# A recurrent attention block and a maxout layer on one core: all engine and load orders laid anew

## The chip, the core and the metric

The kernel runs on one core of a Trainium2 chip. A core has TensorE (PE, matrix products, with its weight loads shown apart as PEld), VectorE (DVE), ScalarE (ACT), GpSimd (POOL) and SyncE (SP, which only issues transfers here). The metric is the device time of one execution in microseconds; the median of three runs of the kernel before is 131.71 us (131.47 to 132.38).

## The reference

Two stages. The first is a gated linear recurrence for 4 batches of 8 heads, 768 steps, head size 48:

```
for t in range(768):
    state = alpha[:, :, t, :, None] * state + einsum('bhd,bhe->bhde', k[:, :, t], v[:, :, t])
    y[:, :, t] = einsum('bhd,bhde->bhe', q[:, :, t], state)
```

Its output, laid out as x with 3072 rows of 384, goes through a layer with 1024 hidden columns:

```
g = maximum(x @ w1, x @ w2)
out = g @ w_out
```

## The kernel before

The 768 steps are cut into chunks of 128, and two chunks of one batch (256 steps) are a *unit*; there are 12 units. The recurrence becomes matrix products: cumulated logarithms of alpha turn q and k into scaled forms, the scores inside a chunk are one masked product, and what older chunks give comes through a running state. The maximum is computed as x @ w2 + relu(x @ (w1 - w2)), so that the second product needs two parts: relu(...) @ w_out and x @ (w2 @ w_out), where w2 @ w_out is computed once at the start.

Names of the steps, with u the unit (units 0 and 1 are cut into two halves of four heads, .0 and .1) and their lines:

- `ld.*` (L346, L368, transposes L515): loads that SP issues; af, qf, kf, vf are alpha, q, k, v of a unit, w2, wo, w1 pieces of the weights. Units 4 to 6 and 11 use the weights' staging space.
- `lg`, `sg`, `ra` (L457 to L465): logarithm of alpha, sum of a step pair, exponential. `cs` (PE, L480, L482): cumulated sums. `em`, `ep`, `de` (ACT, L485 to L489): their exponentials.
- `k0`, `q0`, `kn`, `qn` (L415, L497, L502): scaled k and q. `tp` (PE, L527): their transposes, `qk` (L418): the copy out of PSUM. For units 10 and 11 transposing transfers on SP take the place of both.
- `pp` (PE, L553): scores; `pt` (DVE, L565, L570): scores times the mask.
- `kv` (PE, L602), `tm` (DVE, L635, L637), `dd`, `sb` (L621, L415): update of the running state. `vc`, `w` (L418): copies of v; `dm` (L588): decay factors.
- `y` (PE, L663): output of the recurrence; `xt` (L418): its copy out of PSUM.
- `wt` (PE, L383), `wtc`, `woc` (L418), `wq` (PE, L405), `wqc` (L409): w2 transposed, w_out cast, and the 24 products of w2 @ w_out. `w12` (L399): w1 - w2, in four column groups.
- `h` (PE, L693), `g` (L698 on DVE, L699 on ACT): the hidden product, four column groups per unit, and its relu. `o` (PE, L720), `oc` (L418), `st` (L730, L735): the output product, copy and store (ACT issues it).

Many steps can run on more than one of ACT, DVE and POOL; many helpers share one line (copies L418, products L415).

The order of the work is written out by hand: `ORDERS` holds for each of PE, ACT, DVE, POOL and SP the list of step names in the sequence in which that engine runs them, and with it on which engine a step runs. `Plan.follow` steps through these lists with a duration for every step and constants for latencies, tile-shape switches and instruction fetches. It doesn't reorder anything; from its reckoned times come the PSUM bank that each result takes (`where`), the sequence in which instructions are emitted, and the gaps of PE in its first 45 us, into which `fill` (L840) emits products of a zero tile:

```
while left > 0.06:
    cols = min(512, int(600 * left / slow) - 3)
    nc.tensor.matmul(env["PB"][b][:, 0:cols], lhsT=w[:, 0:128], rhs=w[:, 0:cols], start=True, stop=True)
```

Waits between engines follow from the data. The tile shapes of PE products are three: whole array, A (64 rows: tp, pp, kv) and C (32 columns: y).

Of the kernel before, what the change touches and what calls it, by code (L numbers as in the profile page):

```python
# [201 lines left out]
o1.0.x0 cs4 h2.3 h2.0 h2.2 pp3 cs5 o2.1.x0 o2.0.x0 o2.0.f0 h2.1 o2.1.f0 y3 tpk4 tpq4 o2.1.f1 o2.0.f1 o2.0.f2
o2.1.f2 h3.3 pp4 o2.1.f3 h3.0 h3.2 o2.0.f3 h3.1 tpq5 kv5 tpk5 kv4 o3.0.x0 cs6 o3.0.f0 o3.1.x0 o3.1.f0 o3.0.f1
o3.1.f1 o3.1.f2 o3.1.f3 o3.0.f2 y4 pp5 o3.0.f3 h4.0 h4.3 h4.2 h4.1 y5 tpk6 tpq6 kv6 cs8 cs7 h5.0 o4.0.x0 o4.0.f0
h5.1 o4.0.f1 o4.0.f2 o4.1.x0 o4.0.f3 o4.1.f0 o4.1.f1 tpq7 pp6 tpk7 o4.1.f2 o4.1.f3 h5.3 o5.0.x0 h5.2 o5.0.f0
o5.0.f1 y6 tpk8 tpq8 kv7 o5.0.f2 o5.0.f3 o5.1.x0 o5.1.f0 pp7 o5.1.f1 cs9 h6.0 o5.1.f2 o5.1.f3 h6.2 h6.3 y7 tpq9
tpk9 pp8 o6.1.x0 h6.1 o6.1.f0 h7.3 h7.1 o6.1.f1 kv8 kv9 pp9 o6.1.f2 h7.0 h7.2 o7.0.x0 o7.1.x0 y8 y9 cs10 o7.0.f0
o6.0.x0 o6.0.f0 cs11 o7.1.f0 o7.1.f1 o6.0.f1 h8.2 o7.0.f1 o8.0.x0 o7.0.f2 o6.1.f3 h8.0 o7.0.f3 o7.1.f2 o6.0.f2
h8.1 o6.0.f3 h9.0 h8.3 o8.0.f0 o8.1.x0 h9.3 o7.1.f3 o8.1.f0 h9.1 o8.0.f1 o8.0.f2 kv10 pp10 o8.1.f1 o9.1.x0
o8.1.f2 o8.1.f3 o9.1.f0 o8.0.f3 h9.2 y10 kv11 pp11 o9.1.f1 o9.0.x0 o9.0.f0 o9.1.f2 h10.0 o9.0.f1 o9.0.f2  # L210
o10.0.x0 o10.1.x0 o9.1.f3 o10.0.f0 y11 o10.1.f0 o9.0.f3 h10.2 h10.1 h10.3 h11.0 o10.0.f1 h11.3 h11.1 o10.1.f1
# [11 lines left out]
qk8.1 oc5.0 lg10 vc8 w7.01 em9 ep9 de9 g6.0 g6.2 g6.3 xt7.0 xt7.1 w9.00 qk9.1 w10.11 g6.1 g7.3 st4 g7.1 w9.01
w10.00 st5 lg11 g7.0 w9.10 ra10 ra11 g7.2 xt8.1 de10 xt8.0 em10 ep10 em11 vc11 g8.2 ep11 de11 g8.0 g9.0 w10.10
g8.3 oc6.1 g9.3 g9.1 oc8.1 w11.11 xt10.1 st6 w11.00 g10.0 xt11.0 xt11.1 oc9.1 g11.0 st7 g10.2 g10.3 st8 g11.1
g11.3 oc9.0 st9 st10 oc11.0 st11.0 oc11.1 st11.1 st11.2
# [3 lines left out]
q00.0 qn0.1 kn0.0 qn0.0 kn1.0 k01.1 q01.0 pt0.1.1 qn1.1 qn1.0 pt0.1.0 qk1.0.1 pt0.0.1 tm1.0 pt1.0.0 pt1.0.1  # L230
pt0.0.0 pt1.1.0 tm0.0 pt1.1.1 tm1.1 wtc.20 tm0.1 xt0.1 xt1.1 w12.1 wtc.01 zsb0 w12.2 sg2 w12.3 zsb2 g0.2 g0.3
kn2 g1.3 q02 qn2 dm3 q03 qn3 qk2.0 w2.01 k03 tm2.0 pt2.0 pt2.1 qk3.0 tm3.0 xt2.1 tm2.1 qk3.1 oc1.0 q04 tm3.1
pt3.0 pt3.1 qn4 xt3.0 k05 dm5 sg6 qk4.0 qn5 pt4.0 pt4.1 oc2.1 g3.2 g3.1 tm5.0 tm4.0 sb5.1 sg7 qk5.0 qk5.1 tm5.1
tm4.1 xt4.1 pt5.1 pt5.0 qn6 g4.3 oc3.0 tm6.0 g4.2 qk6.0 qn7 tm6.1 qk6.1 oc4.0 qn8 pt6.0 pt6.1 oc4.1 g5.2 g5.3
# [644 lines left out]
```

## Time and profile before

| | |
|---|---|
| median of 3 runs | 131.71 us |
| profiled execution: span | 129.8 us |
| median less that span | 1.9 us |
| PE busy | 124.4 us (96%) |
| of it fills (L840) | 10.6 us |
| DVE, ACT, POOL busy | 98.6, 96.8, 70.7 us |
| mean granted TensorE clock | 0.999 |
| read from HBM, written | 23.59 MB, 4.72 MB |

The profiled execution's own time beside its span isn't in the profile: the span runs from its first to its last instruction, and what lies around it is taken as the 1.9 us between the span and the median. Busy time of PE comes from matmuls whose ends are modelled, and fills count in it. A row of the stretches gives start and end, length, then the busy time and count of PE, PEld, DVE, ACT and POOL, the granted clock, the share of DMA time and GB/s. A row of the chain of waits gives start, length, engine, tile and line. Rows of the timeline have start, length, engine, line, operation, tiles, shapes, count, and in brackets idle time before it with what ended it.

### The profile page before, as it was taken

The page shows a single profiled execution, that of the slowest core. Times are in us where ns is not written, and L with a number is a line of the kernel's source. Part 1 is how long each engine was busy: PE and PEld are TensorE (multiplying, and loading weights), DVE is VectorE, ACT ScalarE, POOL GpSimd, SP SyncE. Part 2 cuts the span into 40 slices and gives each one's busy share as a digit, 9 for nine tenths or more (in the row PEclk, how much of TensorE's full clock was granted, in tenths as well). Part 3 has the DMA queues.
Part 4 walks back from the last instruction along what each step waited for, and adds up shares of the span by engine and source line. Part 5 has one row for each costly group of instructions (what it writes and reads, how often), then busy time and mean ns, then how long its engine had stood idle before and what let it go on. Part 6 is the DMA issues. An engine that isn't in the chain of part 4 may idle for free.

```text
span 129.8 us, 4785 instructions
## 1 busy us (share of the span) xinstructions
PE 124.4 (96%) x1987; PEld 88.5 (68%) x1987; DVE 98.6 (76%) x177; ACT 96.8 (75%) x199; POOL 70.7 (54%) x112
## 2 busy tenths in 40 slices
...
GB/s 76 325 325 357 414 371 346 344 273 294 232 314 309 262 275 250 318 272 315 301 314 337 251 287 340 202 230 135 5 13 91 105 89 39 121 5 14 258 167 167
DMA packets 60837, 29.66 MB, mean 229 GB/s; under 512 B 54672, under 2 KB 60432, under 8 KB 60816
## 3 DMA queue, kind: packets, MB, share of 16 engines
...
q10 hardware_dynamic: 3424, 4.72, 10.0%
q8 instruction: 15, 0.25, 0.7%
q14 instruction: 6, 0.05, 0.1%
HBM read 23.59 MB, written 4.72 MB: 218 GB/s over the span
## 4 chain that ended last, share of the span: by engine, by line
PE 79%; ACT 9%; DMA 5%; issue 2%; DVE 2%; SPq 0%; ACTq 0%
PE pb L720 28%; PE pb L693 20%; PE pb L840 8%; PE pb L663 6%; DMA af<-in_alpha_dram 5%; PE pb L527 4%; PE pb L553 3%; PE pb L405 3%; PE pb L602 3%; ACT w L418 2%; PE pb L480 1%; ACT ra L465 1%; PE pb L383 1%; ACT gt L699 1%; ACT lg L457 1%
## 5 line engine op out<-in xcount | busy, mean ns | idle before, releaser
L720 PE MATMUL pb<-wo,gt 128*128 128x384 f16 (+2 forms) x200 | 39.8, 320 | 0.0
L693 PE MATMUL pb<-xt,w 128*128 128x256 f16 x288 | 36.7, 272 | 0.1
L693 PEld LDWEIGHTS <-w 128*128 128x128 f16 x288 | 27.9, 98 | 6.5 <-issue 0.4
L699 ACT ACTIVATE gt<-pb 128x512 f16<-128x512 f32 x35 | 20.2, 595 | 9.7 <-PE pb L693 9.1
L565 DVE TENSOR_TENSOR pt<-pb,mask 128x1024 f16<-128x1024 f32 x20 | 23.5, 1217 | 1.9 <-PE pb L553 1.9
L720 PEld LDWEIGHTS <-gt 128*128 128x128 f16 x200 | 18.1, 98 | 9.1
L415 POOL TENSOR_TENSOR sb<-tm,dd 128x384 f16<-128x384 f32 x15 | 12.4, 830 | 9.0 <-DVE tm L635 8.7
L698 DVE TENSOR_SCALAR gt<-pb 128x512 f16<-128x512 f32 x13 | 8.7, 680 | 9.0 <-PE pb L693 9.0
L720 PE MATMUL pb<-w2o,xt 128*128 128x384 f16 (+2 forms) x75 | 15.3, 320 | 0.0
L840 PE MATMUL pb<-wsrc 128*128 128x512 f32 (+6 forms) x18 | 10.6, 709 | 1.5 <-DVE wsrc L846 1.5
L418 ACT CAST xt<-pb 128x384 f16<-128x384 f32 x15 | 8.3, 592 | 4.4 <-PE pb L663 4.3
L635 DVE TENSOR_TENSOR tm<-pb,sb 128x384 f32<-128x384 f32 x16 | 8.6, 550 | 3.6 <-PE pb L602 2.9
L418 DVE COPY os<-pb 128x384 f32<-128x384 f32 (+1 forms) x13 | 6.9, 531 | 4.7 <-PE pb L720 4.5
L418 ACT COPY os<-pb 128x384 f32<-128x384 f32 (+1 forms) x12 | 5.6, 468 | 6.4 <-PE pb L720 5.9
L418 ACT COPY qk<-pb 128x512 f16<-128x512 f16 (+1 forms) x13 | 9.9, 781 | 0.3 <-PE pb L527 0.2
L663 PE MATMUL pb<-pt,w 128*32 128x128 f16 x384 | 10.1, 220 | 0.0
L663 PEld LDWEIGHTS <-w 128*32 128x32 f16 x384 | 8.3, 96 | 2.5 <-issue 1.9
L418 ACT CAST w<-vf 64x384 f16<-64x384 f32 x19 | 9.7, 509 | 0.3
L497 POOL TENSOR_TENSOR kn<-kf,em 128x768 f16<-128x768 f32 (+1 forms) x5 | 8.3, 1650 | 2.6 <-PE pb L553 1.9
L720 PEld LDWEIGHTS <-xt 128*128 128x128 f16 x75 | 6.9, 98 | 4.0
L663 PE MATMUL pb<-qk,sb 128*32 128x128 f16 x240 | 9.5, 219 | 0.0
L457 ACT ACTIVATE lg<-af 128x768 f16<-128x768 f32 (+1 forms) x10 | 6.9, 710 | 3.3 <-DMA af<-in_alpha_dram 3.0
...
## 6 DMA issues: line engine op xcount, KB each, us to landing
out_dram<-os ACTq DMA_DIRECT2D x11, 384.0 KB, 3.0
af<-in_alpha_dram SPq DMA_DIRECT2D x8, 384.0 KB, 6.5
kf<-in_k_dram SPq DMA_DIRECT2D x8, 384.0 KB, 5.8
qf<-in_q_dram SPq DMA_DIRECT2D x8, 384.0 KB, 5.2
vf<-in_v_dram SPq DMA_DIRECT2D x8, 384.0 KB, 5.4
...
wof<-in_moe_w_out_dram SPq DMA_DIRECT2D x4, 384.0 KB, 7.5
w1f<-in_moe_w_dram SPq DMA_DIRECT2D x4, 384.0 KB, 9.2
```

Source lines behind the costliest of these rows:

```text
L415: return lambda: getattr(nc, e).tensor_mul(out=o(), in0=x(), in1=y())
L418: return lambda: nc.scalar.copy(out=o(), in_=i()) if e == "scalar" else getattr(nc, e).tensor_copy(out=o(), in_=i())
L457: add(f"lg{nq}", "ACT", lambda h_=h_: nc.scalar.activation(out=V("LG")[lg][:, :, h_].rearrange("p r h d -> p h r d"), in_=AFn()[:, h_], fu ...
L497: eng.tensor_mul(out=V(nm)[i3][:, :, h_, 0:D], in0=rhd(src())[:, :, h_], in1=bc(fac()))
L565: f = lambda e=e: nc.vector.tensor_mul(out=V("PT")[pt][:, e].rearrange("p a j x -> p (a j) x"), in0=pair(pp[e][0]).rearrange("p n (j x) -> ...
L635: nc.vector.tensor_add(out=V("TM")[new], in0=kvv, in1=V("SB")[m4])
L663: nc.tensor.matmul(o, lhsT=l, rhs=r, start=(a, qd) not in seen, stop=i == len(todo[qd]) - 1, skip_group_check=True)
L693: nc.tensor.matmul(t[:, m, :], lhsT=V("w12")[:, ds, f * 128 : f * 128 + 128], rhs=V("XT")[x3][:, ds, :], start=(ds == 0), stop=(ds == ND - 1))
L698: gd = lambda g2=g2, v2=v2: nc.vector.tensor_relu(out=g2(), in_=v2())
L699: ga = lambda g2=g2, v2=v2: nc.scalar.activation(out=g2(), in_=v2(), func=ACTF.Relu)
L720: nc.tensor.matmul(b32(x, w), lhsT=l, rhs=r, start=fst and y_ == 0, stop=lst and y_ == len(ws) - 1)
L840: nc.tensor.matmul(env["PB"][b][:, 0:cols], lhsT=w[:, 0:128], rhs=w[:, 0:cols], start=True, stop=True)
```

## The change

The five lists in `ORDERS` are replaced by others with the same steps. Every PE step and every load is in both, in another sequence; ACT has 202 entries where it had 212, DVE 176 where it had 165, POOL 100 where it had 101. The constants in `Plan` by which the lists are reckoned change as well: the switch between tile shapes depends on the pair of shapes, an instruction fetch delays the load queue by up to 0.6 us some time after it's asked for, a store's issue takes 0.42 us of ACT where it took 0.1, and some durations differ by a few hundredths. Operations, tiles and data types are as before.

At the start, PE has these steps ahead of the first h: before, nine of the 24 wq, with y1 and y0 in front of all of them; after, eighteen wq, seven of them in front of y0 and y1. The load list puts all four wo pieces ahead of w1.0. `w12.0` moves from POOL to DVE, `sb1.1` from POOL to DVE, `sg1.0` and `k01.0` too. The relu `g` goes from 35 on ACT and 13 on DVE to 27 and 21; output copies from 12 and 13 to 18 and 7; `xt` from 15 and 9 to 19 and 5; of the 48 copies `w`, ACT makes 22 and POOL 23 where they made 32 and 14.

```diff
-    SWITCH = 0.096
+    SWITCH = {"u": 0.112, "A": 0.128, "C": 0.148, "uC": 0.1}
...
-    FETCH = 0.85
+    FETCH = 0.6
+    BACKLOG = (25.0, 3.0, 1.2)
...
     "PE": """
-cs0.1 cs1.1 cs1.0 cs0.0 tpk0.1 tpq0.1 tpq0.0 tpk0.0 pp0.1 tpq1.1 tpk1.0 tpq1.0 tpk1.1 kv1 pp0.0 wt.11 pp1.0
-wt.10 wt.01 pp1.1 kv0 wt.00 wt.21 wt.20 y1.0 y1.1 y0.0 y0.1 wq.10 wq.20 wq.11 wq.21 wq.00 wq.01 wq.22 wq.12
-wq.02 h0.0 h1.0 wq.23 h0.1 h1.1 o1.1.f0 wq.13 h0.2 h1.2 cs2 o1.1.f1 o0.1.f0 wq.03 wq.24 o0.1.f1 h0.3 wq.14 wq.15
...
+cs1.1 cs0.1 cs0.0 cs1.0 tpk0.1 tpq0.1 tpq0.0 tpk0.0 pp0.1 kv0 tpq1.0 tpk1.0 pp0.0 wt.20 tpk1.1 tpq1.1 kv1 wt.21
+wq.20 wt.00 pp1.1 pp1.0 wq.21 wt.10 wt.01 wt.11 wq.00 wq.01 wq.22 wq.02 wq.23 y0.0 y0.1 y1.0 y1.1 wq.03 wq.24 wq.10
+wq.25 wq.26 wq.04 wq.11 wq.12 wq.05 wq.13 wq.06 h1.0 h0.0 wq.27 h1.1 o1.0.f0 h1.2 wq.14 h0.2 o1.1.f0 wq.07 wq.15 cs2
...
     "DVE": """
...
+q00.1 k00.0 qn0.1 qn0.0 kn0.0 qk0.1.0 k01.0 k01.1 kn1.0 pt0.1.1 tm0.0 pt0.1.0 qn1.0 qn1.1 qk1.0.0 pt0.0.0 pt0.0.1
+qk1.1.0 tm1.0 tm0.1 pt1.1.0 pt1.0.0 pt1.1.1 pt1.0.1 sb1.1 woc.5 woc.4 w12.0 zkn2 w12.1 w12.2 g1.2 sg2 tm1.1 g0.2
...
     "SP": """
-ld.af0 ld.af1 ld.kf0 ld.qf0 ld.kf1 ld.vf1 ld.qf1 ld.vf0 ld.w2.1 ld.w2.0 ld.wo.0 ld.w2.2 ld.w1.0 ld.wo.1 ld.w1.1
-ld.w1.2 ld.af2 ld.wo.2 ld.w1.3 ld.kf2 ld.af3 ld.wo.3 ld.qf2 ld.qf3 ld.vf2 ld.kf3 ld.vf3 ld.af4 ld.af5 ld.qf4
...
+ld.af1 ld.af0 ld.kf0 ld.qf0 ld.vf0 ld.kf1 ld.qf1 ld.vf1 ld.w2.2 ld.wo.0 ld.w2.0 ld.w2.1 ld.wo.1 ld.wo.2 ld.wo.3
+ld.w1.0 ld.w1.1 ld.w1.2 ld.af2 ld.af3 ld.w1.3 ld.kf2 ld.qf2 ld.qf3 ld.vf2 ld.kf3 ld.vf3 ld.af4 ld.qf4 ld.kf4 ld.af5
```

More of the change, by code (lines that the diff above doesn't have):

```diff
@@ L80, in follow @@
         count, block, pe = 0, 189, 1.2
-        nblock, avail = 0, 0.0
+        nblock, avail, due = 0, 0.0, []
+        wait = lambda at: due.append(at + self.BACKLOG[1 if at < self.BACKLOG[0] else 2])
         def ready(o):
@@ L149, in follow @@
                     while count >= block:
-                        avail, free["SP"] = pe + late(nblock), max(free["SP"], pe) + self.FETCH
+                        avail = pe + late(nblock)
+                        wait(pe)
                         block, nblock = block + 256, nblock + 1
@@ L156, in follow @@
                     tc = max(tc, avail)
-                    avail, free["SP"] = tc + late(nblock), max(free["SP"], tc) + self.FETCH
+                    avail = tc + late(nblock)
+                    wait(tc)
                     block, nblock = block + 256, nblock + 1
@@ L160, in follow @@
                 pe = t + dur
+            if o.eng == "SP":
+                while due and due[0] <= t + o.dur:
+                    dur += max(0.0, min(self.FETCH, due.pop(0) + self.FETCH - t))
             o.start, o.end = t, t + dur
@@ L202 @@
[L202 to L211, printed above, removed]
@@ new lines @@
+h0.1 wq.16 o0.0.f0 o1.1.f1 wq.17 h0.3 o1.0.f1 h1.3 cs3 o1.0.f2 o0.0.f1 o1.1.f2 o1.0.f3 tpq2 tpk2 o1.1.f3 o1.1.x0
+o0.0.f2 o0.0.f3 kv2 pp2 o0.0.x0 o0.1.f0 o1.0.x0 o0.1.f1 o0.1.f2 tpq3 tpk3 kv3 y2 o0.1.f3 o0.1.x0 pp3 h2.0 cs4 h2.2
+o2.0.x0 h2.3 h2.1 cs5 o2.0.f0 o2.1.x0 o2.1.f0 y3 tpk4 tpq4 o2.1.f1 o2.1.f2 o2.1.f3 o2.0.f1 o2.0.f2 h3.0 pp4 o2.0.f3
+h3.3 cs6 h3.1 kv4 kv5 tpk5 tpq5 h3.2 o3.1.x0 o3.0.x0 o3.0.f0 o3.1.f0 o3.1.f1 o3.1.f2 o3.1.f3 o3.0.f1 o3.0.f2 y4 pp5
+o3.0.f3 cs7 h4.1 h4.2 cs8 o4.1.x0 h4.0 y5 tpk6 tpq6 h4.3 o4.1.f0 o4.0.x0 o4.1.f1 o4.0.f0 o4.1.f2 o4.0.f1 o4.1.f3
@@ new lines @@
+tpq7 pp6 tpk7 o4.0.f2 o4.0.f3 h5.2 h5.3 h5.1 h5.0 kv6 tpk8 kv7 tpq8 cs9 o5.1.x0 o5.1.f0 o5.1.f1 o5.1.f2 o5.1.f3 y6
+pp7 o5.0.x0 o5.0.f0 h6.2 o5.0.f1 h6.1 o5.0.f2 o5.0.f3 h6.0 y7 tpq9 tpk9 pp8 o6.1.x0 h6.3 o6.1.f0 h7.1 h7.3 o6.1.f1
+kv9 kv8 pp9 o6.1.f2 h7.2 cs10 o6.1.f3 o6.0.x0 y8 y9 cs11 o6.0.f0 o6.0.f1 o6.0.f2 o7.0.x0 h8.2 o6.0.f3 h7.0 h8.1 h8.3
+o7.1.x0 o7.1.f0 o7.0.f0 o7.0.f1 o7.1.f1 h8.0 h9.0 o7.0.f2 o7.1.f2 h9.1 o7.1.f3 o7.0.f3 o9.1.x0 kv11 pp10 kv10
+o8.0.x0 o9.0.x0 o9.1.f0 h9.2 o9.0.f0 h9.3 o9.1.f1 o9.0.f1 o9.0.f2 o8.0.f0 pp11 o8.1.x0 o8.0.f1 o9.1.f2 o8.1.f0
@@ L223 @@
[L223 to L226, printed above, removed]
+lg1.1 lg1.0 lg0.1 lg0.0 em1.1 em0.1 de0.1 ra0.1 ra0.0 ep0.1 de1.1 em0.0 em1.0 ep0.0 de0.0 ep1.0 vc0 ra1.0 ra1.1
@@ L227 @@
+ra9 w6.00 oc4.0 vc7 g5.3 g5.1 ra10 g5.0 w8.10 qk8.0 w6.11 oc5.1 em9 de9 xt6.1 ep9 g6.2 w8.11 oc5.0 g6.0 xt7.0 xt7.1
+qk9.0 w9.01 vc9 g6.3 g7.1 g7.3 w9.11 lg11 st5 w9.10 de10 st3 em10 g7.2 st4 xt8.1 w11.00 ep10 xt8.0 xt9.0 em11 de11
+oc6.0 xt9.1 vc11 g8.3 ra11 oc6.1 g8.1 ep11 g9.1 g8.0 oc7.1 xt10.0 st6 xt11.0 st7 oc8.0 xt11.1 g10.0 st8 oc9.1 g10.2
+st9 oc10.1 oc10.0 oc11.0 st10 st11.0 st11.1 st11.2
 """,
     "DVE": """
-zqn0 own zqn1 zsg0 zsg1 zkn2 zqn2 zkn0 trj sg0.1 zw0 ind zkn1 zsb3 sg1.1 sg0.0 zw2 zw1 k00.1 kn0.1 q00.1 k00.0
@@ L230 @@
[L230 to L234, printed above, removed]
@@ L235 @@
-xt6.0 tm7.0 qk8.0 pt7.0 pt7.1 qn9 tm7.1 oc5.1 qk9.0 pt8.0 pt8.1 sb8.0 sb9.0 w8.11 tm9.0 tm8.0 pt9.0 pt9.1 q010
-k010 sg11 xt9.1 qn10 xt9.0 qn11 oc7.0 kn11 oc6.0 g8.1 oc7.1 vc10 sb11.0 tm10.0 pt10.0 pt10.1 oc8.0 g9.2 tm11.0
-xt10.0 sb11.1 pt11.1 pt11.0 g10.1 g11.2 oc10.1 oc10.0 oc11.2
+zkn0 zqn1 zqn2 zsb0 trj zsg1 own zsb2 zw2 zsg0 ind sg1.1 zw0 sg1.0 zw1 sg0.1 zqn0 k00.1 sg0.0 zsb1 kn0.1 q00.0 zkn1
+q00.1 k00.0 qn0.1 qn0.0 kn0.0 qk0.1.0 k01.0 k01.1 kn1.0 pt0.1.1 tm0.0 pt0.1.0 qn1.0 qn1.1 qk1.0.0 pt0.0.0 pt0.0.1
```

59 lines of the change are left out of this document (31 added, 28 removed).

## The prediction

> **What bounds the kernel now.** I read the page's busy table first, then busy time by stretches, then the chain of waits in order of time, then the start of the program engine by engine.
>
> ```profile
> span 129.8 us, 4785 instructions
> PE 124.4 (96%) x1987; PEld 88.5 (68%) x1987; DVE 98.6 (76%) x177; ACT 96.8 (75%) x199; POOL 70.7 (54%) x112
> L840 PE MATMUL pb<-wsrc 128*128 128x512 f32 (+6 forms) x18 | 10.6, 709 | 1.5 <-DVE wsrc L846 1.5
> ```
>
> TensorE (PE) is busy 96% of the span, but 10.6 us of that are the fills of L840, which compute nothing. The stretches say where they lie and when PE becomes the only limit:
>
> ```profile
> 7.68:13.22 5.54, 5.54 (x55) 2.42 (x53) 5.34 (x13) 5.34 (x20) 2.23 (x4) 1.00 1.15 347
> 13.22:19.50 6.28, 5.85 (x121) 4.60 (x124) 6.06 (x12) 6.18 (x14) 5.72 (x15) 1.00 1.05 392
> 22.36:60.00 37.64, 37.55 (x624) 26.93 (x621) 33.79 (x53) 34.74 (x72) 22.79 (x29) 1.00 1.04 288
> 60.00:126.50 66.50, 66.43 (x1092) 49.20 (x1086) 46.65 (x68) 45.05 (x88) 35.16 (x53) 1.00 0.61 169
> ```
>
> From 22.36 us to 126.5 PE has no fill and is short of full by 0.09 + 0.07 us: that part is its own work, at clock 1.00. Before 19.5 us VectorE (DVE) and ScalarE (ACT) are full instead (5.34 of 5.54 us each, then 6.06 and 6.18 of 6.28), and PE fills time. The chain shows the hand-over and the end:
>
> ```profile
> 19.49 1.47 PE pb L663 x88
> 20.96 1.57 PE pb L405 x9
> ...
> 30.14 0.16 PE pb L405
> ...
> 122.23 4.27 PE pb L720 x37
> 126.52 0.29 DVE os L418
> ```
>
> L663 at 19.49 is y of units 0 and 1 (all four halves, 1.47 us); the nine L405 are the first nine wq; then come the first h (L693).
>
> So the end is the moment at which PE last had to wait, plus the PE work then left, plus the 3.3 us of tail from 126.5 (last evacuation and store). The change keeps the work. It can win only by having more of it done when the last early wait ends, and lose by ending that wait later or by a new wait inside the full stretch.
>
> **The change part by part: the first h.** In the kernel before, the first h follows the difference w1 - w2 of its columns (w12.0):
>
> ```profile
> 20.37 1.83 POOL L399 TENSOR_TENSOR w<-w1f,w2f 128x768 f16<-128x768 f32 x1 [0.56 <-DMA w1f<-in_moe_w_dram]
> 22.36 1.47 PE L693 MATMUL pb<-xt,w 128*128 128x256 f16 x12
> ```
>
> GpSimd (POOL) ended it at 20.37 + 1.83 = 22.20, and h0.0 began 0.16 later. In the new PE list 18 of the 24 wq stand ahead of the first h, not 9 (the cs, tp, pp, kv, wt and y ahead of it are the same). One wq alone took 0.16 (30.14); nine of them behind y, with a change of tile shape in front, took 1.57 (20.96), so a change of shape (a switch) is about 0.1 and nine more wq are 1.46. The kernel breaks even if its first h begins at 22.36 + 1.46 = 23.8 us.
>
> That h again waits for w12.0, and so for load w1.0. It was the thirteenth load and becomes the sixteenth: the four w_out pieces now go ahead of it. Landings, from the answers for single issues (start of issue, then time to landing):
>
> ```profile
> L368 SPq DMA_DIRECT2D w2f<-in_moe_w_dram x1: 465/465/465, 11.1 to 11.1; - x1
> ...
> DMA to landing us min/median/max: 6.5/6.5/6.5
> L368 SPq DMA_DIRECT2D w1f<-in_moe_w_dram x1: 432/432/432, 11.6 to 11.6; - x1
> ...
> DMA to landing us min/median/max: 8.6/8.6/8.6
> L368 SPq DMA_DIRECT2D w1f<-in_moe_w_dram x1: 616/616/616, 13.1 to 13.1; - x1
> ...
> DMA to landing us min/median/max: 10.3/10.3/10.3
> wof<-in_moe_w_out_dram SPq DMA_DIRECT2D x4, 384.0 KB, 7.5
> w1f<-in_moe_w_dram SPq DMA_DIRECT2D x4, 384.0 KB, 9.2
> ```
>
> The twelfth load landed at 17.6, the thirteenth at 20.2, the sixteenth (w1.2) at 23.4. Steps 13 to 16 are 1.07 each; the step from 12 to 13 is 2.6, so 1.5 us too long. The w_out and w1 pieces are equally large and the first sixteen loads hold the same bytes in both orders, so I put w1.0 at 23.4. Its difference moves from POOL to DVE, where one takes 0.94:
>
> ```profile
> L399 DVE TENSOR_TENSOR w<-w1f,w2f 128x768 f16<-128x768 f32 x3 | 2.8, 937 | 1.4 <-DMA w1f<-in_moe_w_dram 1.4
> 18.70 0.68 DVE L570 TENSOR_TENSOR pt<-pb,mask 128x512 f16<-128x512 f32 x1
> 20.36 0.55 DVE L635 TENSOR_TENSOR tm<-pb,sb 128x384 f32<-128x384 f32 x1
> 14.04 0.41 DVE L418 COPY qk<-pb 128x512 f16<-128x512 f16 x1
> L415 DVE TENSOR_TENSOR sb<-tm,dd 128x384 f16<-128x384 f32 x5 | 2.7, 546 | 0.0
> L418 ACT CAST wo<-wof 128x384 f16<-128x384 f32 x7 | 3.5, 511 | 1.5 <-DMA wof<-in_moe_w_out_dram 1.5
> ```
>
> 23.4 + 0.1 + 0.94 + 0.16 = 24.6. Two other paths end near there. First, seven wq now stand ahead of y; wq.22 needs the cast of wo.1, the new thirteenth load: 20.2 + 0.1 + 0.51 + 0.16 = 20.9, then three wq 0.5, y 1.5 with a switch, and eleven wq 1.8: 24.7. Second, DVE: its last score mask (pt) ahead of y ended at 18.70 + 0.68 = 19.4; the new list puts two more qk copies (0.82), one tm (0.55) and sb1.1 (0.55) in front of y1, 1.9 us, or 1.7 with the overlap of neighbours: y1 from 21.2, over at 22.0, eleven wq, 23.8. I take 24.6, 0.8 us behind the break-even. The bounds are 23.4 (DVE's path with its 0.2 + 0.2 us of idle time gone) and 25.0.
>
> The 1.5 us is where a rule of the notes speaks.
>
> ```profile
> q8 instruction: 15, 0.25, 0.7%
> ```
>
> Fifteen instruction packets took 0.7% of sixteen engines' span, so 0.7% x 16 x 129.8 / 15 = 0.97 us each on one DMA engine: about the size of that long step. The Trainium skill, Runtime: NRT & Kernel Launch, section Instruction fetch mechanics, has code refilled in 16 KiB blocks, with the crossing of one "mostly hidden". By that page the step would come from elsewhere; the long step does not look hidden. What the landings would be without it is a rival below.
>
> **The rest.** *Tile switches*: from the lists, 51 become 50, -0.1 us. *Kinds of PE work*: unchanged. *Engine shares*: ACT gives up 8 relu, 10 w casts, 3 w_out casts and 2 qk copies and takes 6 output copies and 4 xt; DVE takes the relu and 4 dm and gives up the output copies and xt; POOL takes 9 w casts. From 63 us DVE and ACT have room (46.65 and 45.05 of the last 66.5 us are busy), so a move there is free; before 60 it is not (33.79 and 34.74 of 37.64): a rival. *Later loads*: alpha of units 2 and 3 fall to nineteenth and twentieth place, by steps of 1.1 us to about 26.8 and 27.9; their cs now stand 1.5 and 0 us later in PE's work, so nothing waits. qf2, the twenty-third in both orders, stays. *Transposes of units 10 and 11* on SP (SyncE): behind them stands only each other.
>
> ```profile
> 95.90 1.30 SPq L515 DMA_TRANSPOSE qk<-kn x1
> 105.04 0.49 PE pb L553 x12
> ```
>
> From the first transpose to pp10 (L553) 9.1 us passed, and the four issues it needs take 5.2. By the PE work counted in the lists, pp10 stands 2.3 us earlier and cs10, which starts that chain, 3.3 us earlier. Nothing if this holds, 1 us if not. *End*: the last pieces are the same; oc11.1 goes to DVE and is covered by eleven narrow matmuls, at most 0.3 us if not. *The planner's constants* change only which PSUM banks and how many fills are emitted. *Inside the full stretch* before lost under 0.2 us; a plan of the same kind, just as tight, I give 0.2 more.
>
> Sum: +0.8 - 0.1 + 0.2 = +0.9 us. The span would be 130.7; the median 131.71 lies 1.9 us above the profiled span, so **132.6 us**.
>
> **Rivals.**
>
> *The long step stays away from the new order.* Then w1.0 lands at 21.9, w12.0 is no limit, and DVE's path gives h from 23.4 to 23.8: -0.4 to 0, **131.4 us**. For it: if the step is an instruction packet's, it follows PE's instruction count, which the new order and its fills shift. Against it: in sixteen places there is room for it anyway. The page's "mostly hidden" would lead here. Chance 0.20. To win over 1% h would have to begin by 22.5, before DVE is through y: 0.06 of these.
>
> *DVE becomes the bound after the start.*
>
> ```profile
> 35.00:63.00 28.00, 27.86 (x521) 20.13 (x519) 26.82 (x41) 26.73 (x53) 21.72 (x28) 1.00 1.07 286
> 37.39 2.35 DVE L565 TENSOR_TENSOR pt<-pb,mask 128x1024 f16<-128x1024 f32 x2
> 39.98 0.46 PE L663 MATMUL pb<-pt,w 128*32 128x128 f16 x20
> ```
>
> The masks of unit 2 ended at 39.74 and y2 began at 39.98: no slack to speak of. In the new order DVE stands idle for w1.0 from about 22 (after sb1.1 and two casts) to 23.5, some 1.2 us, with w12 and everything of unit 2 queued behind it, and from 35 to 63 us it is 96% busy and cannot catch up. If that carries to y2, PE waits up to 1.2 us: 131.7 + 0.7 + 1.2 = **133.6 us**. It decides where the masks of unit 2 end later than about 40.5, where PE would want y2. Against it: from 22.36 to 35 DVE idled 2.7 us already. Chance 0.25.
>
> *A planned fill too many*: one of 512 columns is 0.8 us of PE time if its gap is not there: 133.4. Chance 0.05.
>
> The forecast keeps 0.50.
>
> **The numbers.** Within 1% (131.7 +/- 1.3, about what a measurement of this kernel can tell from no change) lie the forecast but for a tail of 0.03 on the slow side, and the first rival but for its 0.06: 0.47 + 0.14 = 0.61; with 0.02 of the second, whose small sizes lie inside, 0.63. Faster 0.06. Slower 0.23 + 0.05 + 0.03 = 0.31. The range goes from the first rival's 131.4 less 0.2 of noise to the second's 133.6 plus 0.3: 131.2 to 133.9.
>
> **What would show it.** Right: w12.0 (L399) on DVE starts near 23.5 directly behind a DMA wait; first L693 near 24.6; PE full from there to about 127.3; tail 3.3. First rival: w1.0 lands before 22.5. Second: PE idle in front of L663 near 40 with DVE pt as releaser. I am wrong if the first h begins before 23.4, or if PE between the first h and its last matmul takes other than 102.6 us (104.2 less 1.46 and 0.1) by more than 0.6.

## The result, and the profile after

The kernel after takes 133.47 us (median of six runs, 133.29 to 135.72) where the kernel before takes 131.81 beside it (six runs, 131.47 to 132.43): a ratio of 1.0137, 95% interval 1.0094 to 1.018. The forecast of 132.6 us was 0.9 us too low; the range held the time. The profiled execution took 133.4 us, 1.7 us more than its span. The ratios leave out runs of over 1.5% above the fastest of their kernel, so some differ from the quotient of the medians.

The page after: the span, the busy table, and the group of the fills.

```profile
span 131.7 us, 4785 instructions
...
PE 123.2 (94%) x1991; PEld 89.5 (68%) x1991; DVE 102.8 (78%) x189; ACT 90.3 (69%) x189; POOL 66.2 (50%) x110
...
L845 PE MATMUL pb<-wsrc 128*128 128x512 f32 (+8 forms) x22 | 8.4, 494 | 1.5 <-DVE wsrc L851 1.5
```

Lines of the kernel after are five higher than before for these steps: y is L668, h L698, o L725, wq L410, wt L388, fills L845. The stretches of the same kernel, with the columns as before:

```profile
13.22:19.50 6.28, 5.30 (x86) 3.98 (x87) 4.35 (x10) 4.43 (x9) 4.62 (x11) 0.73 1.04 396
19.50:24.60 5.10, 5.10 (x115) 3.94 (x116) 4.43 (x10) 4.41 (x10) 1.01 (x2) 1.00 1.11 345
24.60:35.00 10.40, 9.40 (x80) 7.00 (x79) 8.40 (x12) 7.38 (x16) 3.44 (x3) 1.00 1.03 277
35.00:63.00 28.00, 27.79 (x542) 19.48 (x541) 26.23 (x43) 25.98 (x53) 21.00 (x29) 1.00 1.06 286
63.00:100.00 37.00, 37.00 (x738) 28.22 (x736) 32.38 (x49) 30.95 (x64) 27.29 (x41) 1.00 0.78 211
```

Two rows have no counterpart before: the granted clock is 0.73 between 13.22 and 19.50, and PE is idle for 1.0 us between 24.60 and 35.00. The chain of waits (start, length, what) passes through both:

```profile
10.65 7.14 DMA w2f<-in_moe_w_dram
...
17.93 1.00 PE pb L388 x4
18.93 0.55 PE pb L558 x16
...
21.87 1.47 PE pb L668 x88
23.34 1.90 PE pb L410 x11
...
30.48 0.82 DVE w L404
...
31.90 1.96 DVE sg L465
...
36.45 0.64 PE pb L532 x32
...
125.06 3.45 PE pb L725 x31
```

First, load w2.0 lands at 10.65 + 7.14 = 17.79; from there PE works without a break (5.10 of the 5.10 us from 19.50 on) through the transposes of w2 (L388), the scores of unit 1 (L558), wq, y (L668) from 21.8 and eleven more wq to the first h: 25.07 in the timeline below, not 24.6. Second, from 28.4 to 36.4 the chain runs over DVE, with a sum of logarithms (L465, sg3) of 1.96 us that takes 0.35 elsewhere. From 36.45 it is PE to the last matmul, which ends at 125.06 + 3.45 = 128.51.

So the 1.9 us between the spans are: the first h 2.71 us later (25.07 against 22.36), less 1.46 for the nine wq that already lie behind it, 1.25; and from the first h to the last matmul 128.51 - 25.07 = 103.44 where the forecast had 102.6, 0.8; the tail is 0.1 shorter. The prediction had called itself wrong for more than 0.6 us of difference in that second part: there, by its own sign, it is wrong.

The timeline of PE after shows where the clock was lost (in brackets the idle time ahead and what ended it):

```profile
14.06 0.29 PE L532 MATMUL pb<-ident,qn 64*128 64x64 f16 x8 [2.07 <-DVE qn L502]
...
14.62 0.66 PE L388 MATMUL pb<-ident,w2f 128*128 128x128 f32 x4
...
16.35 1.11 PE L388 MATMUL pb<-ident,w2f 128*128 128x128 f32 x4
...
17.93 1.00 PE L388 MATMUL pb<-ident,w2f 128*128 128x128 f32 x4
...
25.07 1.47 PE L698 MATMUL pb<-xt,w 128*128 128x256 f16 x12
```

PE stood idle for 2.07 us, with no fill in that gap: the plan emits fills only where a PSUM bank is free for a whole gap, and here none was. The same four transposes then take 0.66 us once and 1.1 and 1.0 afterwards. And the timeline of DVE and POOL after, around 31 us:

```profile
30.39 1.58 DVE L404 TENSOR_TENSOR w<-w1f,w2f 128x768 f16<-128x768 f32 x1
31.90 1.96 DVE L465 TENSOR_TENSOR sg<-lg 128x384 f16<-128x384 f16 x1
...
30.16 1.00 POOL L420 TENSOR_TENSOR kf<-kf,af 128x384 f32<-128x384 f32 x1 [8.84 <-DMA kf<-in_k_dram]
31.33 2.31 POOL L502 TENSOR_TENSOR kn<-kf,em 128x768 f16<-128x768 f32 x1 [0.17 <-ACT em L490]
```

DVE's w12.3 ran 1.58 us (0.94 is usual) over POOL's k02, and sg3 did not end before POOL's kn2 had (31.33 + 2.31 = 33.64). PE's cs3 and tpq2 stand behind these steps. The plan knows this hold: `follow` lets a DVE step marked `sh` start only when POOL's step is over (`port` holds POOL in turn), and by its reckoning sg3 is over at 29.58 us, before kn2 starts at 31.07. In the trace kn2 starts 0.3 us later than planned, but sg3 2.6 us later, because DVE is already 1.7 us late at w12.0, which waits for w1.0 (23.52, planned 21.80).

### The profile page after: what moved, and what is told of

It is laid out like the page before. It is cut to its first block, busy times and chain, and to the rows that moved or that the text cites. A ratio compares the mean times of both kernels' runs of the same rounds, so it can differ in the third digit from the quotient of the medians.

```text
span 131.7 us, 4785 instructions
## 1 busy us (share of the span) xinstructions
PE 123.2 (94%) x1991; PEld 89.5 (68%) x1991; DVE 102.8 (78%) x189; ACT 90.3 (69%) x189; POOL 66.2 (50%) x110
## 4 chain that ended last, share of the span: by engine, by line
PE 78%; SPq 7%; DVE 5%; DMA 5%; issue 1%; DVEq 0%
PE pb L725 32%; PE pb L698 22%; PE pb L668 7%; SPq L351 6%; DMA w2f<-in_moe_w_dram 5%; PE pb L558 4%; PE pb L532 3%; PE pb L607 3%; PE pb L410 2%; PE pb L388 2%; DVE sg L465 2%; DVE gt L703 1%; SPq L373 1%; PE pb L485 1%; DVE qn L502 1%
## 5 line engine op out<-in xcount | busy, mean ns | idle before, releaser
L725 PE MATMUL pb<-wo,gt 128*128 128x384 f16 (+2 forms) x200 | 38.0, 320 | 0.0
L698 PE MATMUL pb<-xt,w 128*128 128x256 f16 x288 | 37.0, 273 | 0.3 <-DVE w L404 0.3
L698 PEld LDWEIGHTS <-w 128*128 128x128 f16 x288 | 27.6, 98 | 6.6 <-DVE w L404 0.7
L725 PEld LDWEIGHTS <-gt 128*128 128x128 f16 x200 | 18.3, 98 | 9.5
L704 ACT ACTIVATE gt<-pb 128x512 f16<-128x512 f32 x27 | 15.6, 597 | 7.7 <-PE pb L698 7.7
L703 DVE TENSOR_SCALAR gt<-pb 128x512 f16<-128x512 f32 x21 | 14.2, 684 | 7.2 <-PE pb L698 7.2
L423 ACT CAST xt<-pb 128x384 f16<-128x384 f32 x19 | 10.6, 595 | 10.1 <-PE pb L668 10.0
L420 POOL TENSOR_TENSOR sb<-tm,dd 128x384 f16<-128x384 f32 x17 | 14.0, 828 | 3.4 <-DVE tm L640 2.9
L725 PE MATMUL pb<-w2o,xt 128*128 128x384 f16 (+2 forms) x75 | 15.3, 320 | 0.0
L423 ACT COPY os<-pb 128x384 f32<-128x384 f32 x18 | 8.4, 478 | 8.8 <-PE pb L725 8.7
L423 ACT COPY qk<-pb 128x1024 f16<-128x1024 f16 (+1 forms) x11 | 8.9, 810 | 1.8 <-PE pb L532 1.8
L668 PEld LDWEIGHTS <-w 128*32 128x32 f16 x384 | 8.4, 96 | 2.4 <-issue 1.7
L668 PE MATMUL pb<-pt,w 128*32 128x128 f16 x384 | 10.0, 220 | 0.0
L845 PE MATMUL pb<-wsrc 128*128 128x512 f32 (+8 forms) x22 | 8.4, 494 | 1.5 <-DVE wsrc L851 1.5
L668 PE MATMUL pb<-qk,sb 128*32 128x128 f16 x240 | 9.4, 219 | 0.0
L725 PEld LDWEIGHTS <-xt 128*128 128x128 f16 x75 | 6.7, 97 | 3.8
L423 POOL CAST w<-vf 64x384 f16<-64x384 f32 x16 | 8.3, 522 | 0.8
L420 POOL TENSOR_TENSOR kf<-kf,af 128x384 f32<-128x384 f32 x4 | 4.0, 1000 | 8.9 <-DMA kf<-in_k_dram 8.8
```

The costliest lines, as they stand in the source:

```text
L420: return lambda: getattr(nc, e).tensor_mul(out=o(), in0=x(), in1=y())
L423: return lambda: nc.scalar.copy(out=o(), in_=i()) if e == "scalar" else getattr(nc, e).tensor_copy(out=o(), in_=i())
L668: nc.tensor.matmul(o, lhsT=l, rhs=r, start=(a, qd) not in seen, stop=i == len(todo[qd]) - 1, skip_group_check=True)
L698: nc.tensor.matmul(t[:, m, :], lhsT=V("w12")[:, ds, f * 128 : f * 128 + 128], rhs=V("XT")[x3][:, ds, :], start=(ds == 0), stop=(ds == ND - 1))
L703: gd = lambda g2=g2, v2=v2: nc.vector.tensor_relu(out=g2(), in_=v2())
L704: ga = lambda g2=g2, v2=v2: nc.scalar.activation(out=g2(), in_=v2(), func=ACTF.Relu)
```

## The experiments

In kernels with an edited list, banks and fills are those reckoned from the unedited lists, so that the edit is the only difference. Times are medians; ratios, with their 95% intervals, are against the kernel before on the same chip.

**1. The DVE steps set apart from POOL's.** The kernel after, with w12.3 and sg3 ahead of POOL's k02 and kn2, and k02 itself on DVE.

```diff
 DVE
-sg2 tm1.1 g0.2 w12.3 sg3 g0.1 q02 g0.3 qn2
+sg2 g0.2 w12.3 g0.1 tm1.1 sg3 q02 k02 qn2 g0.3
 POOL
-w1.11 k02 kn2
+w1.11 kn2
```

> The changed kernel with the banks of every result kept, but on VectorE unit 0's g0.2, w12.3, g0.1 and the sums of unit 3 drawn ahead, and k02 moved from GpSimd to VectorE, so that w12.3 and sg3 run while GpSimd has no product. Theory (two engines hold each other up between 30 and 34 us: w12.3 took 1.59 for 0.96, sg3 1.96 for 0.36): w12.3 under 1.0 us, sg3 under 0.4, PE's idle time between 24.6 and 35 us falls from 1.0 to at most 0.3, and the time falls by 1.0 to 1.3, to about 132.2. Rival (VectorE is simply behind by its wait for w1.0): both steps get short but PE waits as long in front of later steps, and the time stays within 0.3 of 133.4.

Measured: 133.6 us, ratio 1.0132 (1.0092 to 1.0171). Its stretches, and PE's only wait of over 0.1 us after 24 us:

```profile
24.60:35.00 10.40, 10.40 (x98) 7.78 (x98) 8.40 (x14) 8.00 (x19) 1.58 (x1) 1.00 1.01 277
35.00:63.00 28.00, 26.86 (x534) 18.77 (x527) 26.99 (x41) 26.28 (x52) 21.70 (x30) 1.00 1.04 282
```

```profile
PE pb L500 <- DVE xt L438: 1.0, 1, 1.0
```

w12.3 took 0.95 and sg3 0.35, and PE is full from 24.60 to 35.00: the collision was what cost the 1.0 us there. But PE lost 1.1 us between 35 and 63, at cs7, behind three DVE steps that were stretched in turn beside POOL (sb4.1, sg8 and dm6: 1.11, 1.16 and 0.90 us for 0.55, 0.35 and 0.18), and the time is the same. The gain was given back.

**2. A fill in the gap.** The kernel after with one fill planned for 12 to 14 us.

```diff
-    ... for t0, t1, b in P.gaps(45.0, 0.25)]
+    ... for t0, t1, b in P.gaps(45.0, 0.25) + [(11.96, 13.88, 1)]]
```

> The changed kernel with one more fill, in PE's gap between kv0 and tpq1.0 (2.07 us idle at 12.0 to 14.06, no fill was emitted there). Theory (that gap lowers the granted clock, 0.73 between 13.2 and 19.5 us, and the slow transposes of w2 put the start back): clock 1.00 there, four transposes of w2 in 0.44 us instead of 0.9, wt.00 still held by its load to 17.9, first h at about 24.6 instead of 25.07, time -0.5: 132.9. If the later holds between VectorE and GpSimd at 30 to 34 us hang on how late PE is, up to another 0.5 goes: 132.4. Rival (the clock costs nothing, because the loads of w2 set the start): clock 1.00, first h and time unchanged, 133.4 +/- 0.2.

Measured: 133.34 us (132.5 to 136.34, twelve runs), ratio 1.0107 (1.0066 to 1.0147). The slow stretch, and the transposes of w2.0 and the first h in PE's timeline:

```profile
13.22:19.50 6.28, 5.04 (x93) 3.43 (x92) 4.91 (x11) 4.45 (x8) 4.63 (x11) 1.00 1.04 395
```

```profile
17.74 0.63 PE L388 MATMUL pb<-ident,w2f 128*128 128x128 f32 x4 [1.04 <-DMA w2f<-in_moe_w_dram]
...
24.54 0.71 PE L698 MATMUL pb<-xt,w 128*128 128x256 f16 x5
```

The clock is 1.00, the first h begins at 24.54 instead of 25.07, and PE now waits openly for w2.0. The five later kernels that keep this fill and this order of the start (experiments 7, 8, 9, 11 and 12) have the first h between 24.43 and 24.75; the two without the fill, after and experiment 1, at 25.07 and 25.06. So the fill is worth 0.3 to 0.6 us at the first h. In the time it isn't shown: the interval overlaps that of the kernel after, and the profiled execution is the shortest of the twelve.

**3. The reverse: before without its late fills.** In the kernel before, the fills after pp0.1 left out.

```diff
-    ... for t0, t1, b in P.gaps(45.0, 0.25)]
+    ... for t0, t1, b in P.gaps(45.0, 0.25) if t0 < 11.0]
```

> The kernel before without the fills that follow pp0.1 (1.6 us at 11.6 to 13.2). Theory (an unfilled gap of this length lowers the clock some 2 us later): granted clock between 13.2 and 19.5 us falls from 1.00 to 0.7 to 0.9, transposes of w2 take up to twice their 0.109 us each, first h 0.3 to 1.0 us after 22.36, time 132.1 to 132.8. Rival (fills there buy nothing): clock and time as before, 131.8 +/- 0.3.

Measured: 132.43 us, ratio 1.0055 (1.0019 to 1.0091). PE's timeline and the stretch behind it:

```profile
13.52 0.29 PE L527 MATMUL pb<-ident,qn 64*128 64x64 f16 x8 [1.43 <-DVE qn L497]
```

```profile
13.22:19.50 6.28, 5.92 (x105) 4.84 (x106) 5.24 (x11) 6.02 (x13) 5.22 (x14) 0.73 1.05 389
```

An idle gap of 1.43 us was enough for the same 0.73, and the first h came at 23.50, 1.14 us later, although w1.0 landed 1.5 us earlier than in the kernel before (18.75 against 20.21). The fills do none of the kernel's work, yet leaving them out costs 0.6% of its time.

**4. The constants alone.** The lists of before with the planner's new constants.

```diff
-    SWITCH = 0.096
+    SWITCH = {"u": 0.112, "A": 0.128, "C": 0.148, "uC": 0.1}
...
```

> The lists of the kernel before with the planner's new constants. They can touch only banks, the columns of the fills and the emission sequence across engines. Expected: the time of before within 0.4 us (131.4 to 132.2). Rival (new banks add waits): over 132.4, with PE idle after 22 us.

Measured: 131.87 us, ratio 0.9997 (0.997 to 1.0024). The constants change nothing by themselves; the lists do. The clock between 13.22 and 19.50 is 1.00 here, so the gap without a fill comes from the lists as well.

**5. Places in the load queue.** The kernel before with three w_out pieces ahead of w1.0.

```diff
-ld.w2.2 ld.w1.0 ld.wo.1 ld.w1.1 ld.w1.2 ld.af2 ld.wo.2 ld.w1.3 ld.kf2 ld.af3 ld.wo.3
+ld.w2.2 ld.wo.1 ld.wo.2 ld.wo.3 ld.w1.0 ld.w1.1 ld.w1.2 ld.af2 ld.w1.3 ld.kf2 ld.af3
```

> The kernel before with the load order alone changed: wo.1, wo.2 and wo.3 ahead of w1.0, which so becomes the sixteenth load as in the kernel after (before it was the thirteenth). Theory: a load lands by its place, w1.0 at 23.4 us; w12.0 on POOL ends at 25.3, the first h begins at 25.5 instead of 22.36 (+3.1), nothing else can fill PE, and the time is 134.3 to 135.2 us. Rival: the landing of the thirteenth load is tied to w1.0 itself or the work behind makes up for some of it: under +2 us, below 133.8 us.

Measured: 135.92 us, ratio 1.028 (1.0209 to 1.0352). w1.0 landed at 23.37 and the first h began at 25.39, both as expected; the time lies above the range given because the wait itself brought the clock down, as PE's timeline shows (twelve such matmuls took 1.47 before):

```profile
25.39 2.60 PE L707 MATMUL pb<-xt,w 128*128 128x256 f16 x12 [2.99 <-POOL w L413]
```

The four runs show what that costs: three with a mean clock of 0.987 took 135.90 to 136.01 us, the fourth, at 1.00, took 134.12.

**6. Where the long load step falls.** The kernel after with the fill of experiment 2 and without the six small fills. That puts off PE's 190th instruction, from which the plan reckons the first refill of its code, by some 2 us.

```diff
-    ... P.gaps(45.0, 0.25)]
+    ... P.gaps(45.0, 0.25) + [(11.96, 13.88, 1)] if t1 - t0 > 1.0]
```

> The kernel after with the planned fill at 12 to 14 us and without the six small fills of under 1 us, so that PE reaches its 190th instruction about 2 us later (near 14 us instead of 11.8). Theory (the long step of the loads is the first instruction refill that comes into their way): w2.0, the eleventh load, lands near 16.3 us instead of 17.79, the long step of about 2.6 us falls on a later load (wo.1 to wo.3), and w1.0 still lands near 23.4; first h between 24.3 and 24.7 us; time as with the fill alone, 132.6 to 133.4 us. Rival (the step belongs to w2.0 or to its place): w2.0 lands at 17.8 again.

Measured: 134.62 us, ratio 1.0194 (1.0131 to 1.0256). The rows of single issues (start of the issue behind the commas, then time to landing), w2.0 and wo.1 in this kernel:

```profile
L373 SPq DMA_DIRECT2D w2f<-in_moe_w_dram x1: 466/466/466, 10.6 to 10.6; - x1
DMA to landing us min/median/max: 5.6/5.6/5.6
...
L373 SPq DMA_DIRECT2D wof<-in_moe_w_out_dram x1: 443/443/443, 11.6 to 11.6; - x1
DMA to landing us min/median/max: 8.5/8.5/8.5
```

w2.0 landed at 16.28 (17.79 in the kernel after), the long step (2.6 us) fell two places later on wo.1 (20.17), and w1.0 came at 23.41 as ever. The first h began at 24.69, as the expectation had it; w2.0 was no longer the limit, but wq.22 now waited 1.3 us for the cast of wo.1. The time was worse than expected: PE then lost 1.3 us of the 28 between 35 and 63 and 0.8 after that.

The traces also hold the instruction packets (queue q8) one by one. In the views of DMA traffic by windows, first the kernel after from 14.8 to 16.0 us, then this one from 17.4 to 18.6, then experiment 3 from 18.5 to 19.7:

```profile
q8 instruction: 1, 0.02, 5.4%
```

```profile
q8 instruction: 1, 0.02, 5.8%
```

```profile
q8 instruction: 1, 0.02, 5.8%
```

Before that packet there is none from 9 us on. It stands at the start of the long step each time: w2.0 (15.05 to 17.79) in the kernel after, wo.1 (17.57 to 20.17) here, and in experiment 3 wo.1 again, there the fourteenth load (18.75 to 21.09). In the kernel before it lies between 17.1 and 18.3, and the step is w1.0's (17.61 to 20.21). So the long step moves with the fills, and the packet with it. That the packet makes the step is likely, not shown: six of the seven such packets between 14 and 64 us of the kernel after have a load step of 2.0 to 2.8 us beside them or right behind, but the one near 24.6 has none.

**7. Both cures together.** Experiments 1 and 2 in one kernel.

> The kernel after with both earlier edits at once: the planned fill at 12 to 14 us, and DVE's w12.3 and sg3 set ahead of the stretch in which POOL's k02 and kn2 run (k02 itself on DVE). Theory: the start gives 0.5 us (first h near 24.5 instead of 25.07) and the stalls of 30 to 35 us are gone (1.45 us), but DVE is the bound from 35 to 63 us and takes back most of the second: PE is busy under 27.3 of the 28 us there, and the time is 132.5 to 133.4 us. Rival (the two costs are simply added, and nothing else is late): PE is busy over 27.7 of the 28 us, and the time is 131.4 to 132.0 us.

Measured: 134.22 us, ratio 1.0105 (1.0043 to 1.0167), runs from 132.15 to 135.87. The profiled execution took 135.72 us, 3.6 more than the shortest, so it shows where time can be lost, not what every execution loses. First DVE, then POOL and PE, in its timeline:

```profile
61.32 1.79 DVE L608 TENSOR_TENSOR de<-ex,own 128x32 f32<-128x32 f32 x1
...
61.14 1.92 POOL L517 TENSOR_TENSOR kn<-w1f,em 128x768 f16<-128x768 f32 x1
...
63.67 0.45 PE L500 MATMUL pb<-sg,tri 128*128 128x384 f16 x1 [2.00 <-DVE xt L438]
```

The two costs don't add: the start and the stretch to 35 us are mended (first h at 24.75, PE busy 10.34 of 10.40 behind it), and PE loses 2.0 us at 61.7 instead. dm6 (L608), 32 columns that take 0.18 us alone, lasted 1.79, to the end of POOL's kn6.

**8. Less work for DVE.** As 7, with dm4, dm6, sg8 and sb4.1 moved from DVE to POOL.

```diff
 DVE
-sg6 dm4 tm3.1 ... qn6 sb4.1 tm5.1 tm4.1 k07 sg8 dm6 xt4.1
+sg6 tm3.1 ... qn6 tm5.1 tm4.1 k07 xt4.1
 POOL
-sg5 kn4 ... dd4.1 w5.01 dd5.1 sb5.1 k06 sg7 kn6 dd6.0
+sg5 dm4 kn4 ... dd4.1 sb4.1 w5.01 dd5.1 sb5.1 k06 sg7 sg8 kn6 dm6 dd6.0
```

> As the run with both edits, and DVE relieved of four steps between 48 and 62 us: dm4, dm6, sg8 and sb4.1 (together about 1.3 us at their undisturbed lengths) go to POOL. Theory (DVE's work is what holds PE from 35 to 63 us): PE's wait for DVE near 62 us is gone or under 0.3 us, PE is busy over 27.6 of the 28 us, and the time is 0.6 to 1.2 us under that of the run with both edits, 131.5 to 132.3 us. Rival (it is not the sum of DVE's work but its two-operand steps being held beside POOL): more POOL work holds DVE as long, PE is busy under 27.4, and the time is within 0.4 us of the run with both edits.

Measured: 133.01 us, ratio 1.0123 (1.0075 to 1.0171). The median is 1.2 us under that of experiment 7, but 131.5 to 132.3 was not reached and the ratio is no lower (1.0123 against 1.0105), so a gain is not shown. The profiled execution took 135.12 us, 2.1 more than the median. Its stretch, and POOL and PE in its timeline:

```profile
35.00:63.00 28.00, 25.80 (x505) 18.21 (x499) 23.39 (x36) 26.09 (x51) 21.49 (x30) 1.00 0.98 265
```

```profile
56.40 1.00 POOL L439 TENSOR_TENSOR w1f<-w1f,ra 128x384 f32<-128x384 f32 x1 [2.35 <-DMA w1f<-in_q_dram]
...
62.03 0.24 PE L687 MATMUL pb<-pt,w 128*32 128x128 f16 x4 [2.08 <-DVE tm L659]
```

DVE had 4.6 us to spare and PE lost 2.2 all the same: POOL waited for the load of q of unit 6, and sb4.1, now behind it on POOL, held y4. In that execution it isn't the sum of DVE's work that holds PE; the moved step made the new wait, so the run doesn't say what a relief without one would bring.

**9. The copy that PE waits for put first.** As 7, with xt4.1 ahead of sg8 and dm6.

```diff
-tm4.1 k07 sg8 dm6 xt4.1
+tm4.1 k07 xt4.1 sg8 dm6
```

> The run with both edits, and on DVE the copy xt4.1, for whose PSUM bank cs7 waited 2.0 us at 61.7, set ahead of sg8 and dm6; the same work on every engine. Theory (PE is not held by the sum of DVE's work but by single DVE steps that end only with the POOL step beside them, where PE needs what stands behind): sg8 and dm6 are still stretched beside POOL's kn6 (over 1 us each, 0.35 and 0.18 alone), but cs7 no longer waits for them; PE is busy over 27.7 of the 28 us from 35 to 63, and the time falls by 1 to 2 us against the run with both edits, to 131.2 to 132.0 us. Rival (DVE has too much work up to 63 us): the wait comes back within the next 3 us at another step, PE is busy under 27.0, and the time stays above 132.4 us.

Measured: 137.41 us, runs from 134.1 to 138.5, ratio 1.0186 (1.0139 to 1.0232), which rests on the two shortest runs, 134.1 and 134.32. A miss. In the profiled execution, of 138.23 us, cs7 no longer waited, but ten us earlier pp4 did. DVE idled 2.04 us for kf5, which landed at 50.44 (48.5 in run 7), and then dm4 was held to the end of POOL's kn5:

```profile
50.47 0.56 DVE L436 TENSOR_TENSOR w2f<-w2f 128x384 f32<-128x384 f32 x1 [2.04 <-DMA w2f<-in_k_dram]
...
51.21 1.80 DVE L609 TENSOR_TENSOR de<-ex,own 128x32 f32<-128x32 f32 x1
...
51.16 1.81 POOL L518 TENSOR_TENSOR kn<-w2f,em 128x768 f16<-128x768 f32 x1 [3.15 <-ACT os L439]
...
54.73 0.75 PE L574 MATMUL pb<-qk 48*128 48x128 f16 x16 [3.10 <-DVE qk L439]
```

**10. A start laid by the traced landings.** As 9, without small fills, w1.0 fourteenth, y ahead of every product of wo.1, twelve wq ahead of the first h; on DVE and ACT the casts of wo.2 and wo.3 come later.

```diff
 SP
-ld.wo.1 ld.wo.2 ld.wo.3 ld.w1.0 ld.w1.1 ld.w1.2
+ld.wo.1 ld.w1.0 ld.wo.2 ld.w1.1 ld.wo.3 ld.w1.2
 PE
-wq.00 wq.01 wq.22 wq.02 wq.23 y0.0 y0.1 y1.0 y1.1 ...
+wq.00 wq.01 wq.10 wq.11 y0.0 y0.1 y1.0 y1.1 wq.22 wq.02 wq.23 wq.03 wq.12 wq.13 h1.0 h0.0 ...
```

> As the run with xt4.1 moved, and a start laid by the traced landings: no fill of under 1 us (so that the long step of the loads falls behind w2.0, as in the run without small fills), w1.0 fourteenth instead of sixteenth with wo.2 and wo.3 behind it, y of units 0 and 1 ahead of every product that needs wo.1, 12 wq ahead of the first h, and the casts of wo.2 and wo.3 behind w12.0 and the first relu. Theory: w1.0 lands at 21.2 us, w12.0 ends at 22.3, the first h begins at 22.5; break-even for 12 wq is 22.36 + 3 x 0.163 = 22.85, so 0.3 us is won at the start; with no other wait the time is 130.9 to 131.6 us, under both kernels. Rival (the long step goes with w1.0 or the later part stalls anew): first h after 23.2 or PE busy under 27.5 of the 28 us from 35 to 63, and the time is 132 us or more.

Measured: 134.58 us, ratio 1.0204 (1.0162 to 1.0246). w1.0 landed at 21.10 as expected, but the first h began at 23.61: y waited 0.96 us for a copy of w2 transposed that stands on ACT behind the cast of wo.1. Later PE lost 1.7 us between 35 and 63, again with dm4 held on DVE (1.81 us), and 1.5 us more up to 100. On ACT I had left two copies of w2 transposed behind the cast of wo.1, a load that y itself doesn't need.

**11 and 12. q and k of unit 6, then also k of unit 5, earlier in the load order.** As 9, with

```diff
-ld.af7 ld.kf7 ld.qf6 ld.af9 ld.af8 ld.kf6
+ld.af7 ld.qf6 ld.kf6 ld.af8 ld.kf7 ld.af9
```

and in the second also kf5 ahead of af6.

> As the run with xt4.1 moved (fill at 12 to 14 us, w12.3 and sg3 ahead of POOL's steps), and in the load order q and k of unit 6 two places earlier: qf6, kf6, af8, kf7, af9 in place of kf7, qf6, af9, af8, kf6. Theory (from 25 to 63 us the load stream is full, a load lands by its place, 1.2 us each, and POOL's k06 and kn6 begin when kf6 lands): kf6 lands near 56.3 us instead of 58.9 to 60.4, POOL's kn6 ends before 61.9, PE does not wait between 56 and 63 us, and where kf5 lands before 49 us PE is busy over 27.5 of the 28 us from 35 to 63 and the time is 131.3 to 132.3 us. Rival (the landing of kf6 is covered and DVE's or POOL's own work sets the pace): PE still waits 1 us or more between 56 and 63 us, and the time stays above 132.8 us.

> As the run with q and k of unit 6 earlier, and kf5 one place earlier, ahead of af6. Theory: kf5 lands 1.2 us earlier than it does in the other run, near 47.2 us (49.2 if a long step of the loads falls ahead of it); DVE's k05, for which DVE idled 2.0 us in the run with xt4.1 moved, no longer waits for it, pp5 no longer waits for DVE at 51 us, and the time is 0 to 1.5 us under the other run's and spreads less, 131.2 to 132.2 us. Rival (af6, now one place later, holds ACT, or the landing isn't what DVE waits for): a wait of 1 us or more at 49 to 54 us remains, and the time is within 0.4 us of the other run or above it.

Measured: 134.01 us, ratio 1.0151 (1.0096 to 1.0206) for the first; 134.39 us, 1.0179 (1.0129 to 1.0229) for the second. kf6 landed at 53.40 instead of 58.76 to 60.4 in the first, earlier than the 56.3 expected, and PE was busy 27.42 of the 28 us, 27.69 in the second, where it was 24.78 in the long execution of experiment 9. DVE didn't wait for kf5 in either, so its earlier place had nothing to gain. But the time didn't follow, because PE's wait only moved, to 62.5 us. In the timeline of the first, DVE, POOL and PE:

```profile
61.15 1.95 DVE L482 TENSOR_TENSOR sg<-lg 128x384 f16<-128x384 f16 x1
...
60.20 0.91 POOL L485 TENSOR_TENSOR sg<-lg 128x384 f16<-128x384 f16 x1 [1.15 <-ACT lg L479]
61.07 1.82 POOL L519 TENSOR_TENSOR kn<-w1f,em 128x768 f16<-128x768 f32 x1
...
63.73 0.81 PE L715 MATMUL pb<-xt,w 128*128 128x256 f16 x6 [1.19 <-DVE os L440]
```

POOL's kn6 was no longer held by the load but by a logarithm on ACT, fell on the same 61 to 63 us, held sg8 again, and PE lost its 1.2 us there. In the second the same wait ends at 64.13, and another of 1.20 us at 74.47.

The load stream itself, from 30 to 64 us, first before and then after (packets, MB, share of 16 engines):

```profile
q1 hardware_dynamic: 23972, 9.06, 100.7%
...
q1 hardware_dynamic: 24310, 9.19, 101.5%
```

It is full in both kernels. Each load lands by its place, mostly 1.1 to 1.3 us after the one ahead of it, and 2.0 to 2.4 us after where a long step falls in.

## Why the prediction was right or wrong

**The first h (forecast 24.6, +0.8; measured 25.07, +1.25).** The landings held: w1.0 at 13.1 + 10.3 = 23.4, by place, in the kernel after and in experiment 5. w12.0 ran on DVE from 23.52 to 24.48, behind a wait for its load, as forecast, but wasn't the last wait. The step that failed is the path through wq.22 and y, put at 24.7: it was reckoned from wo.1 and from DVE's masks as they had ended before, and left out w2.0, which moved from tenth to eleventh place and met the long step. And the sentence on the planner's constants, that they change only banks and the number of fills, costed at nothing what a missing fill does: 2.07 us of idle PE, then about 3.4 us at half clock (6.28 x 0.27 / 0.50, with the 0.73 of that stretch). The fill alone brings the first h to between 24.43 and 24.75 (experiment 2), still by way of w2.0. That this path ends, at full clock, where the forecast's other paths do is luck; with the fill and w2.0 early (experiment 6) the first h came at 24.69, now by way of wo.1 and wq.22 as the forecast had reckoned it.

**Inside the full stretch (forecast +0.2 less 0.1 for tile switches; measured +0.8).** This term was mis-sized; the 0.2 was a guess that the new lists would be as tight as the old. PE waited for DVE three times between 24.6 and 36.5, 1.2 us in all by the view of waits, where before it lost 0.2 us up to its last matmul. Some 0.2 to 0.3 us was regained elsewhere; where is not located, and tile switches can't be told apart in it.

**The second rival, DVE as the bound (0.25, 133.6 us).** It gave the measured time nearly, and its cause was half right: DVE idles for w1.0 (0.67 us, 1.2 forecast), and w12 and unit 2 queue behind. Its place, y2 near 40 us, was wrong; no wait stands there. That its 133.6 us came so near is luck. What the runs show instead is DVE held by POOL: experiment 1 takes the collision apart and PE is full to 35 us. The Trainium skill, SBUF — State Buffer, section SBUF: two separate sides, has DVE and GpSimd share a port pair: of a DVE step with two SBUF inputs and a GpSimd step that reads SBUF, the one that starts first takes it for the whole instruction, while the other "fully blocks". The traces agree: sg3 1.96 us against 0.35 (after), sg8 1.95 (experiment 11), dm6 1.79 against 0.18 (experiment 7), each over within 0.3 us of the POOL step beside it.

**The first rival, the long step staying away (0.20).** It didn't: in sixteen places there was room for it, as argued. Wherever it falls, an instruction packet stands at its start (experiment 6). "Mostly hidden", the word of the Trainium skill's Runtime: NRT & Kernel Launch, section Instruction fetch mechanics, doesn't hold for the loads beside it, if the step is that refill's: it costs the load queue some 1.5 us.

**The rest.** The constants alone changed nothing (experiment 4). Nothing waited for alpha of units 2 and 3; PE is full from 63 us to its last matmul, so the transposes of units 10 and 11 cost nothing; the tail is 3.2 us. A planned fill too many did not occur; one too few did.

**What stays open.** No version beat the kernel before. Every run that mended a part of the first 35 us lost PE time again between 35 and 65: at cs7 (experiments 1 and 7), at y4 (8), at pp4 (9 and 10), at an h (11 and 12). In that stretch the load stream is full, DVE and ACT are over 90% busy in the kernels before and after, and a DVE step beside POOL can take 1.6 us more. That the gain is given back there is shown for experiments 1 and 11; the profiles of 7, 8 and 9 are of executions 2 to 4 us longer than the middle of the runs behind their ratios. That one of the three alone sets the pace is not shown: an earlier kf6 ended its wait and brought nothing (11), and the relief of DVE made a new wait (8). The plan reckons with the hold between DVE and POOL, but in the kernel after its time for sg3 is off by 2.6 us; lists reckoned anew from the traced times weren't tried.
